# A gated linear attention and a maxout feed-forward on one core: all step lists and PSUM rooms in another order, with 154 runs of one tile shape on the array instead of 190

## The chip, the cores and the metric

The kernel runs on one core of a Trainium2 chip. The metric is the device time of one launch in microseconds (us); for the time before, it is the median of three runs. TensorE (PE in the profile, its weight loads PEld), VectorE (DVE), ScalarE (ACT), GpSimd (POOL) and SyncE (SP) each work through a list of their own in order, and wait for each other by semaphores.

## The reference

Two blocks follow each other. The first is a gated linear attention (4 batches, 8 heads, 768 steps, 48 features a head); its state has complex gates:

```
mag = sqrt(a_re^2 + a_im^2);  scale = min(mag, 0.999) / (mag + 1e-6);  a = (a_re, a_im) * scale
for t in range(S):
    S_re, S_im = a_re[t]*S_re - a_im[t]*S_im + outer(k[t], v[t]),  a_re[t]*S_im + a_im[t]*S_re
    y[t] = q[t] @ S_re
```

The second takes the heads side by side as 3072 tokens of 384 features:

```
h = max(max(x @ w1, x @ w2), x @ w3)      # 384 -> 768
out = h @ w_out                           # 768 -> 384
```

The activations are fp32. The four weight matrices come in as 64-bit floats.

## The kernel before, in words

The kernel is one program without loops. A text, `SCHEDULE`, lists some two thousand *words*, each a step and a group, such as `U01:5`. The program walks the list and records each word's instructions; a helper class ties each instruction to the one before it on its engine, so the order of the words is the order on every engine. (That is why nearly every row of the profile has one line, that of the helper.)

There are 12 groups. A group is 128 steps of two batches, x and y, so a word such as `Ax:5` belongs to batch x of group 5. The words by kind:

- Loads: `Lr Li Lk Lq Lv` (gates, keys, queries, values), on SyncE's queue.
- Gates, on ScalarE and VectorE: `sqr sqi add lnL expw expe lne relu Lnop abs addw lnw expL mulai mulw stt xor half atan turn`. They give each gate's log size and its angle. `Lnop`, `addw` and `Cd` add by a transfer in memory from GpSimd's queue, unless VectorE does it.
- Running sums over a group, on TensorE: `cs` of the angles and `sums` and `F` of the log sizes; `t nf af sa sb` make sines, `En Ek Eq f0..f3` exponentials out of them.
- `mk mq uk uq` scale the keys and queries, `tpk tpq` turn them on TensorE, `Kc Qc` copy the result out of PSUM, `Q1 Q2 KB QB QG` scale parts of it.
- Scores `A` and `B` on TensorE; `g0..g3` (VectorE) and `b0 b1` (ScalarE) write them through masks into `atm`. `dk` and `h0..h3` keep the state. `y` is the attention's output, and `x` copies it to where the second block reads it.
- Weights: twelve blocks are loaded (`WL`) and made into fp32 out of 64 bits: `Wa` copies the upper half into 16-bit floats (ScalarE or VectorE, as the list `OTHER` says), `We` joins in the lower bits (VectorE), and `Wg` adds the first matrix's negative to the two others. So the maximum is taken over two products and zero, and the first matrix's share goes into a matrix of its own (`T t M m`).
- Second block: up words `U01 U11 U02 U12` (9 products of 128x128 weights and 256 columns each; the small ones of group 0, with an x or y, have 6 of 128 columns), `u..` take the maximum. The down projection is done in seven half-size products `P1`..`P7` with sums of the operands `S1`..`S4` on VectorE, and `Px Py` for what is left; `r1 r6 r75 r57 ox oy` put the output together, `D` stores it.

TensorE's array is used in five tile shapes: 128x128 (up words, P, Px, the weights' products), 128x32 (A, B, y), 128x64 (`cs`), 64x64 (`F sums dk`) and 64x128 (`tpk tpq`). Words of one shape that stand behind each other in TensorE's list are called a run.

PSUM is divided into four rooms of two banks. `SLOTS` has a digit for each word that takes a room, in the order of the words; a word waits until the room's last user has been read. `QUARTERS` names words whose products are each made in four, 32 columns of the weights at a time, with the same columns streamed (for `cs`: in 32s instead of 64s):

```
def mmf(out, lhsT, rhs, **kw):
    for o in range(0, P, 32) if T["word"] in QUARTERS else ():
        mm(out=out[o:o + 32], lhsT=lhsT[:, o:o + 32], rhs=rhs, **kw)
    if T["word"] not in QUARTERS:
        mm(out=out, lhsT=lhsT, rhs=rhs, **kw)
```

In the kernel before, `QUARTERS` is empty.

Of the kernel before, what the change touches and what calls it, by code (L numbers as in the profile page):

```python
# [29 lines left out]
0624060202264204602604204624604602204600406204240620420460246260246202460246024062624640406204602602  # L30
6402466024240642460246026042064264064240246060206426040260046024240604204060420602640424062420242002
4202
"""

OTHER = set("""
Zf:0 Zg:0 afx:0 relu:1 Qcy:0 addw:2 Lnop:2 Wg8:0 u21y:0 addw:3 relu:4 afx:3 abs:4 Lnop:4 u01:2 xx:3 afy:4 afx:5 addw:6 u01:4 afx:6 afy:6 abs:7 relu:8 Kcy:6 afy:7 afx:7 relu:9 abs:9 u11:7 u01:7 afx:9 Kcx:9 xy:8 u11:8 Kcy:9 afy:10 abs:11 Kcx:10 Qcy:10 Kcy:11 Kcx:11 xy:11 u01:11 u11:11
""".split())

QUARTERS = set("""
""".split())  # L40

ROOMS = {0: "w1", 3: "w2", 6: "wo", 11: "w1", 1: "w2", 9: "H", 10: "S", 2: "H", 4: "S", 5: "H", 7: "S", 8: "H"}
# [927 lines left out]
```

## Time and profile before

| | before |
|---|---|
| median of 3 runs | 555.67 us (555.03 to 556.41) |
| profiled execution, its own time | 555.11 us |
| its span in the profile | 553.4 us |
| TensorE busy, share of the span | 524.8 us, 95% |
| VectorE | 470.8 us, 85% |
| ScalarE | 369.7 us, 67% |
| GpSimd | 70.7 us, 13% |
| products in the trace (passes; an fp32 product is two) | 10086 |

The span begins with the first instruction and ends with the last; 1.7 us of the profiled execution's time lie around it. A row of a group has the line, the engine, the operation, what it writes and reads, the count, the busy time and the mean of one in ns, and the idle time before such instructions with what ended it. In a row of the timeline stand start and length in us, the engine, the form and how many of it were merged. A busy PE row includes the time in which a product waits in the array's pipeline, so the starts of two rows tell more than the lengths.

### The profile page before, as it was taken

To read this page: it belongs to the slowest core of one execution; us is meant where nothing else is said; L and a number is where in the kernel's file an instruction comes from. 1 tells how busy PE (TensorE), PEld (TensorE's weight loads), DVE (VectorE), ACT (ScalarE), POOL (GpSimd) and SP (SyncE) were. 2 spreads that over 40 slices of the span, in tenths; PEclk is the share of its full clock that TensorE was granted. 3 is DMA by queue.
4 is the path that set the end of the run, shared out by engine and by line. 5 is a ranking of instruction groups with operands and counts; after the bars stand their busy time and mean duration, and the time that the engine had idled before them with its cause. 6 is when DMAs were issued, how large, how long until landed. Compare 5 with 4: busy or idle time off the path is not lost.

```text
span 553.4 us, 22672 instructions
## 1 busy us (share of the span) xinstructions
PE 524.8 (95%) x10086; PEld 449.1 (81%) x10086; DVE 470.8 (85%) x728; ACT 369.7 (67%) x653; POOL 70.7 (13%) x117
## 2 busy tenths in 40 slices
PE   3579899999999999999999999999999999999996
...
GB/s 227 272 236 195 168 125 80 51 128 63 108 40 122 69 67 53 61 44 89 80 111 58 35 102 129 64 91 52 67 123 18 32 107 70 3 31 2 31 1 28
...
## 3 DMA queue, kind: packets, MB, share of 16 engines
...
q14 instruction: 18, 0.15, 0.1%
...
## 4 chain that ended last, share of the span: by engine, by line
PE 84%; ACT 5%; SPq 5%; DVE 2%; DMA 2%; issue 1%; DVEq 0%; ACTq 0%
PE up L107 33%; PE op L107 24%; PE y L107 7%; PE A L107 5%; SPq L107 5%; PE tp L107 4%; PE dk L107 3%; PE cs L107 3%; PE sums L107 2%; PE F L107 2%; PE B L107 1%; DMA ar<-in_a_re_dram 1%; ACT L L107 1%; ACT L107 1%; DMA ai<-in_a_im_dram 1%
## 5 line engine op out<-in xcount | busy, mean ns | idle before, releaser
L107 PE MATMUL up<-xhx,w 128*128 128x256 f32 x792 | 177.0, 382 | 0.1
L107 PEld LDWEIGHTS up<-xhx,w 128*128 128x128 f32 x792 | 148.9, 190 | 21.2 <-PE B L107 0.3
L107 ACT ACT_TABLE_LOAD x49 | 62.9, 1283 | 1.6 <-PEq L954 0.8
L107 ACT COPY atm<-B 32x128 f32<-32x128 f32 x96 | 24.5, 255 | 36.6 <-DVE atm L107 19.1
L107 PE MATMUL op<-wo,xhx 128*128 128x192 f32 (+1 forms) x220 | 48.6, 364 | 0.0
L107 DVE TENSOR_TENSOR Q<-Q,f 112x1024 f32<-112x1024 f32 (+1 forms) x48 | 45.4, 953 | 2.1 <-ACT Q L107 1.2
L107 POOL DMA_DIRECT2D ar<-nf x40 | 34.6, 1304 | 60.5 <-DVE ar L107 49.2
L107 ACT ACTIVATE f<-F 48x232 f32<-48x232 f32 x96 | 34.4, 359 | 10.3 <-PE F L107 6.3
L107 PEld LDWEIGHTS op<-wo,xhx 128*128 128x128 f32 x220 | 36.5, 190 | 4.8 <-issue 0.8
L107 PE MATMUL y<-atm,vb 128*32 128x64 f32 x1152 | 39.3, 222 | 0.1
L107 PE MATMUL y<-QG,g 112*32 112x64 f32 x1408 | 38.1, 219 | 0.3 <-issue 0.3
L107 PEld LDWEIGHTS y<-atm,vb 128*32 128x32 f32 x1152 | 32.5, 110 | 5.4 <-issue 2.9
L107 PEld LDWEIGHTS y<-QG,g 112*32 112x32 f32 x1408 | 34.9, 110 | 0.5 <-issue 0.5
L107 DVE TENSOR_TENSOR ot<-ot,op 128x384 f32<-128x384 f32 (+1 forms) x56 | 25.6, 465 | 10.7 <-PE op L107 6.4
L107 PE MATMUL op<-wo,strassen 128*128 128x192 f32 x176 | 33.0, 331 | 0.0
L107 POOL DMA_DIRECT2D Ln<-e x9 | 8.3, 923 | 192.0 <-ACT e L107 73.7
L107 DVE COPY_PREDICATED atm<-masko,A 128x256 f32<-128x256 uint8 x72 | 31.3, 436 | 1.7
L107 PE MATMUL op<-w,strassen 128*128 128x192 f32 x176 | 32.2, 329 | 0.0
L107 PE MATMUL A<-Q,K 112*32 112x80 f32 x1536 | 31.6, 234 | 0.2 <-DVE Q L107 0.2
L107 PEld LDWEIGHTS A<-Q,K 112*32 112x32 f32 x1536 | 27.3, 110 | 3.0 <-issue 1.6
L107 ACT COPY Q<-tp 112x1024 f32<-112x1024 f32 x22 | 22.3, 1015 | 10.7 <-PE tp L107 10.6
L107 PEld LDWEIGHTS op<-wo,strassen 128*128 128x128 f32 x176 | 28.8, 190 | 0.8
(149 smaller groups left out, 1071.5 us busy)
## 6 DMA issues: line engine op xcount, KB each, us to landing
...
```

Source lines behind the costliest of these rows:

```text
L107: ins = f(*a, **kw)
```

## The change

No step is changed: the same words are recorded, each once. What changes is data at the head of the file: the order of the words in `SCHEDULE`; the rooms in `SLOTS`; the words that `OTHER` gives to the other of two engines (among them seven of the twelve copies `Wa`, now on VectorE); and `QUARTERS`, which now names 51 words. With the new order TensorE's list falls into 154 runs of one shape instead of 190. `ROOMS` and all functions stay as they are.

```
 SCHEDULE = """
-Lrx:0 sqr0:0 Lix:0 sqi0:0 add0:0 lnL0:0 expe0:0 expw0:0 lne0:0 relu0:0 Z0:0 Z1:0 WL0:0 Liy:0 Wa0:0 sqi1:0 Zf:0 Lry:0 sqr1:0 WL3:0 Lqy:0 Lry:1 WL6:0 WL9:0 Lkx:0
...
-P7:11 r75:11 ox:11 P4:11 Dx:11 r57:11 oy:11 Dy:11
+Zg:0 Lix:0 sqi0:0 Lrx:0 sqr0:0 Zf:0 add0:0 lnL0:0 xor0:0 Liy:0 sqi1:0 expe0:0 Lry:0 sqr1:0 WL0:0 WL3:0 expw0:0 relu0:0
...
+Py:11 P4:11 S1:11 S2:11 P6:11 P5:11 P2:11 S4:11 P3:11 Dx:10 r1:11 Dy:10 r6:11 r75:11 r57:11 ox:11 Dx:11 oy:11 Dy:11
 SLOTS = """
-0240624024202406402024604642064262624062046420640426240260620406404624624620620260264064262464046042
...
+0246246206246026042624046460206402064020462046240620462462024620642064260426042060460642620462640260
...
 OTHER = set("""
-Zf:0 Zg:0 afx:0 relu:1 Qcy:0 addw:2 Lnop:2 Wg8:0 u21y:0 addw:3 relu:4 afx:3 abs:4 Lnop:4 u01:2 xx:3 afy:4 afx:5 addw:6 u01:4 afx:6 afy:6 abs:7 relu:8 Kcy:6 afy:7 afx:7 relu:9 abs:9 u11:7 u01:7 afx:9 Kcx:9 xy:8 u11:8 Kcy:9 afy:10 abs:11 Kcx:10 Qcy:10 Kcy:11 Kcx:11 xy:11 u01:11 u11:11
+Zg:0 Zf:0 Z1:0 Wa3:0 afx:0 ty:0 relu:1 Wa6:0 Qcx:0 Wa9:0 Wa11:0 Wa10:0 addw:2 Wa7:0 xy:0 Wa8:0 Wg8:0 afx:1 afy:2
+u21y:0 relu:3 addw:3 xx:1 xy:1 Qcy:2 addw:4 relu:5 afx:4 abs:5 r1:2 addw:5 Kcx:4 u11:3 tx:5 afx:5 xx:4 Qcx:5 afy:6
+abs:7 addw:7 xy:5 u01:5 Qcy:6 tx:7 afy:7 r1:5 xx:6 xy:6 afy:8 afx:8 abs:9 u11:7 ty:9 afy:9 r1:7 Kcx:9 ty:10 relu:11
+abs:11 addw:11 Lnop:11 tx:11 afy:11 afx:11 r1:9 xy:10 Qcy:11 xy:11 r1:10 u11:11 u01:11 r1:11
 """.split())
 QUARTERS = set("""
+csx:0 csy:0 csx:1 csx:2 Px:3 Py:3 csx:6 P6:4 Px:4 Py:6 Px:6 P3:6 csx:9 csy:9 P7:7 P5:7 P2:7 P4:7 U11:8 csx:10 Px:8
+csy:10 P7:8 U12:9 U02:9 csy:11 Px:9 P6:9 csx:11 P4:9 P2:9 P3:9 Py:10 Px:10 P2:10 P4:10 Px:11 P6:10 U12:11 U11:11 P3:10
+U02:11 U01:11 P7:11 P1:11 Py:11 P4:11 P6:11 P5:11 P2:11 P3:11
 """.split())
```

More of the change, by code (lines that the diff above doesn't have):

```diff
@@ new lines @@
+Zg:0 Lix:0 sqi0:0 Lrx:0 sqr0:0 Zf:0 add0:0 lnL0:0 xor0:0 Liy:0 sqi1:0 expe0:0 Lry:0 sqr1:0 WL0:0 WL3:0 expw0:0 relu0:0
+lne0:0 add1:0 lnL1:0 expe1:0 Lnop0:0 Fx:0 lne1:0 sumsx:0 abs0:0 pw0:0 half0:0 expw1:0 f0x:0 relu1:0 f1x:0 xor1:0
+Lnop1:0 Ekx:0 Eqx:0 abs1:0 Z0:0 Wa0:0 f3x:0 lnw0:0 expL0:0 Z1:0 Wa3:0 Enx:0 We3:0 We0:0 half1:0 mulai0:0 mulw0:0 pw1:0
+lnw1:0 stt0:0 expL1:0 mulw1:0 atan0:0 mulai1:0 stt1:0 turn0:0 Lix:1 Lqx:0 mqx:0 atan1:0 turn1:0 csx:0 csy:0 Lry:1
+Lrx:1 WL6:0 sqr:1 Lkx:0 mkx:0 tx:0 nfx:0 afx:0 Liy:1 sqi:1 add:1 sbx:0 sax:0 ukx:0 WL9:0 Lky:0 WL11:0 lnL:1 f2x:0
@@ new lines @@
+uqx:0 ty:0 expe:1 relu:1 tpkx:0 Kcx:0 Wa6:0 lne:1 tpqx:0 Qcx:0 Fy:0 Wa9:0 QGx:0 nfy:0 sumsy:0 f0y:0 expw:1 xor:1
+kEnx:0 We9:0 Lry:2 We6:0 WL10:0 Eny:0 abs:1 T1:0 half:1 Q2x:0 Eky:0 Eqy:0 Wa11:0 Wa10:0 We10:0 mky:0 f1y:0 Lnop:1 CL:0
+f2y:0 f3y:0 pw:1 Lvy:0 t1:0 T0:0 t0:0 We11:0 T2:0 M0:0 M1:0 t2:0 M2:0 WL1:0 Lqy:0 Liy:2 Lix:2 Lrx:2 Lvx:0 afy:0 lnw:1
+expL:1 mulw:1 say:0 Cdx:0 mulai:1 sqi:2 mqy:0 Wa1:0 QBx:0 stt:1 sby:0 atan:1 We1:0 Q1x:0 Ax:0 KBx:0 sqr:2 add:2 lnL:2
+m0:0 m1:0 uky:0 uqy:0 Cdy:0 turn:1 WL2:0 Wa2:0 g0x:0 g1x:0 Wg1:0 tpky:0 tpqy:0 Qcy:0 We2:0 Wg2:0 Kcy:0 g2x:0 Q1y:0
@@ new lines @@
+Q2y:0 xor:2 csy:1 Z2:0 g3x:0 WL4:0 Wa4:0 We4:0 Wg4:0 kEny:0 dkx:0 expe:2 relu:2 csx:1 tx:1 nfx:1 expw:2 abs:2 half:2
+Cdx:1 Ay:0 ty:1 nfy:1 Z4:0 h1x:0 Lix:3 Bx:0 b0x:0 b1x:0 yx:0 Z3:0 WL5:0 Wa5:0 Lqx:1 Lkx:1 WL7:0 afy:1 xx:0 U01x:0
+addw:2 g0y:0 QBy:0 Cdy:1 g1y:0 h2x:0 g2y:0 We5:0 Wg5:0 dky:0 lnw:2 expL:2 g3y:0 KBy:0 mulw:2 By:0 h3x:0 sby:1 U11x:0
+b0y:0 b1y:0 QGy:0 mulai:2 stt:2 Lqy:1 h1y:0 yy:0 say:1 Wa7:0 h2y:0 h3y:0 xy:0 We7:0 Wg7:0 atan:2 u01x:0 turn:2 sumsx:1
+Ekx:1 sumsy:1 Eqy:1 mqy:1 u11x:0 WL8:0 mkx:1 Wa8:0 Eqx:1 We8:0 Eky:1 uqy:1 lne:2 U01y:0 Wg8:0 U02y:0 u01y:0 Enx:1
@@ new lines @@
+Eny:1 csy:2 ty:2 nfy:2 u02y:0 Fx:1 mqx:1 Lky:1 mky:1 f3x:1 f0x:1 afx:1 sax:1 uky:1 afy:2 sbx:1 U12y:0 U11y:0 u11y:0
+f1x:1 f2x:1 u12y:0 ukx:1 uqx:1 U21y:0 U22y:0 u21y:0 u22y:0 tpky:1 Kcy:1 tpkx:1 Kcx:1 kEnx:1 tpqx:1 tpqy:1 Lnop:2
+kEny:1 Liy:3 Lvx:1 Liy:4 Lvy:1 Oy:0 Qcx:1 QBx:1 Q2x:1 dkx:1 Q1x:1 oy:0 Qcy:1 sqi:3 Fy:1 f0y:1 f3y:1 J3:0 QGx:1 Ax:1
+h0x:1 h1x:1 h2x:1 h3x:1 Lky:2 g0x:1 g1x:1 KBx:1 f2y:1 f1y:1 Q1y:1 g2x:1 g3x:1 h0y:1 Q2y:1 U21x:0 u21x:0 Fx:2 f2x:2
+f0x:2 f1x:2 sumsx:2 dky:1 h1y:1 f3x:2 Ekx:2 Enx:2 Lix:4 Eqx:2 h2y:1 Lry:3 Lrx:3 sqr:3 add:3 xor:3 Bx:1 b0x:1 b1x:1
@@ new lines @@
+U12x:0 u12x:0 lnL:3 relu:3 U22x:0 u22x:0 U02x:0 h3y:1 Ay:1 Lqx:2 Lqy:2 Lkx:2 Lvy:2 KBy:1 csx:2 yx:1 QBy:1 mqx:2 tx:2
+nfx:2 u02x:0 expw:3 By:1 Ox:0 QGy:1 Lrx:4 g0y:1 g1y:1 expe:3 afx:2 abs:3 half:3 g2y:1 g3y:1 mkx:2 addw:3 say:2 b1y:1
+xx:1 b0y:1 sax:2 sbx:2 sby:2 lnw:3 uqx:2 h0x:2 J1:0 Lry:4 yy:1 xy:1 Lvx:2 expL:3 sumsy:2 Fy:2 ukx:2 mulai:3 ox:0 Eky:2
+mky:2 Eny:2 Eqy:2 mqy:2 U11:1 Dy:0 lne:3 Lnop:3 f3y:2 f2y:2 f0y:2 f1y:2 uqy:2 tpqx:2 u11:1 uky:2 tpqy:2 tpkx:2 tpky:2
+mulw:3 stt:3 Qcx:2 Qcy:2 atan:3 Kcy:2 kEny:2 Q1x:2 kEnx:2 Kcx:2 KBx:2 Cdx:2 QBx:2 Cdy:2 turn:3 QGx:2 U01:1 Q2y:2 U12:1
@@ new lines @@
+u01:1 U02:1 u12:1 S3:1 Q2x:2 sqi:4 sqr:4 add:4 Q1y:2 u02:1 csy:3 lnL:4 csx:3 ty:3 nfy:3 tx:3 h0y:2 Ax:2 afy:3 nfx:3
+sbx:3 Ay:2 Dx:0 S1:1 g0x:2 g1x:2 g2x:2 g3x:2 Bx:2 QBy:2 expe:4 P7:1 P1:1 b1x:2 b0x:2 g0y:2 S2:1 afx:3 sax:3 say:3 Px:1
+P5:1 Lqy:3 dkx:2 relu:4 sby:3 g1y:2 g2y:2 J2:0 g3y:2 P6:1 h1x:2 h2x:2 Lrx:5 yx:2 r1:1 KBy:2 h3x:2 By:2 Lix:5 Lry:5
+Lvy:3 Lkx:3 expw:4 abs:4 r6:1 xor:4 r75:1 r57:1 QGy:2 half:4 S4:1 J4:0 Py:1 xx:2 P2:1 addw:4 b0y:2 b1y:2 sumsx:3 Enx:3
+sumsy:3 Eqy:3 dky:2 Eky:3 Ekx:3 Lvx:3 Lky:3 lnw:4 Eny:3 h1y:2 mky:3 P4:1 P3:1 ox:1 mqy:3 oy:1 h2y:2 yy:2 Eqx:3 xy:2
@@ new lines @@
+Fx:3 f2x:3 uky:3 Fy:3 f0y:3 f1y:3 f2y:3 expL:4 U01:2 f3y:3 f3x:3 f1x:3 lne:4 f0x:3 Lqx:3 mqx:3 uqx:3 tpqx:3 uqy:3
+mkx:3 h3y:2 ukx:3 mulai:4 mulw:4 u01:2 stt:4 Qcx:3 Q1x:3 QBx:3 atan:4 tpqy:3 tpky:3 kEny:3 tpkx:3 Kcx:3 Cdy:3 Cdx:3
+turn:4 Kcy:3 Lnop:4 sqr:5 Liy:5 sqi:5 Lvx:4 U02:2 KBx:3 U11:2 Bx:3 Q2x:3 kEnx:3 u02:2 Qcy:3 add:5 h0x:3 Q2y:3 S3:2
+h0y:3 Ax:3 g0x:3 g1x:3 g2x:3 u11:2 g3x:3 Lqx:4 b0x:3 b1x:3 QGx:3 U12:2 dkx:3 dky:3 sumsx:4 Ekx:4 Eqx:4 u12:2 S1:2
+Q1y:3 h1x:3 h1y:3 KBy:3 S2:2 h2x:3 h2y:3 P1:2 P7:2 P5:2 Lky:4 Enx:4 h3y:3 h3x:3 QBy:3 lnL:5 expe:5 csy:4 ty:4 csx:4
@@ new lines @@
+tx:4 Lry:6 Dx:1 mqx:4 nfy:4 expw:5 relu:5 sby:4 nfx:4 afx:4 sbx:4 abs:5 Ay:3 yx:3 By:3 afy:4 g0y:3 g1y:3 g2y:3 xx:3
+sax:4 say:4 P6:2 Py:2 P4:2 S4:2 Px:2 P2:2 Lkx:4 mkx:4 g3y:3 Dy:1 lne:5 r1:2 r6:2 QGy:3 Lqy:4 Lnop:5 addw:5 b0y:3 lnw:5
+ukx:4 b1y:3 uqx:4 r75:2 r57:2 expL:5 P3:2 ox:2 oy:2 Lrx:6 Liy:6 xor:5 half:5 mulw:5 yy:3 xy:3 tpkx:4 tpqx:4 Qcx:4
+mulai:5 stt:5 Fx:4 f3x:4 f0x:4 sumsy:4 Eqy:4 mqy:4 uqy:4 Dx:2 Eky:4 mky:4 Kcx:4 Eny:4 Dy:2 U01:3 U02:3 Lix:6 f1x:4
+sqr:6 uky:4 U11:3 Lvy:4 u01:3 sqi:6 kEnx:4 f2x:4 QBx:4 Q1x:4 tpky:4 tpqy:4 KBx:4 Q2x:4 xor:6 add:6 u02:3 kEny:4 atan:5
@@ new lines @@
+lnL:6 expe:6 u11:3 Qcy:4 Kcy:4 Ax:4 U12:3 QGx:4 g0x:4 Cdx:4 Cdy:4 turn:5 g1x:4 g2x:4 h0x:4 g3x:4 Bx:4 b0x:4 Fy:4 f1y:4
+u12:3 S3:3 Lky:5 b1x:4 f3y:4 f2y:4 f0y:4 dkx:4 Fx:5 h1x:4 h2x:4 f0x:5 h3x:4 f1x:5 h0y:4 S1:3 csy:5 csx:5 f2x:5 f3x:5
+tx:5 nfx:5 dky:4 sumsx:5 ty:5 Eqx:5 Enx:5 P1:3 P5:3 KBy:4 h1y:4 h2y:4 QBy:4 h3y:4 nfy:5 Q1y:4 afx:5 Q2y:4 Ekx:5 expw:6
+yx:4 xx:4 QGy:4 S2:3 Px:3 Py:3 By:4 Ay:4 g0y:4 sbx:5 afy:5 g1y:4 S4:3 g2y:4 P7:3 P6:3 sax:5 relu:6 abs:6 say:5 sby:5
+g3y:4 P2:3 P3:3 half:6 Lqx:5 Lrx:7 Liy:7 Lry:7 h0x:5 mqx:5 uqx:5 b1y:4 b0y:4 yy:4 xy:4 sumsy:5 Lqy:5 r1:3 addw:6
@@ new lines @@
+tpqx:5 lnw:6 Eky:5 Qcx:5 Lqx:6 Lvx:5 r6:3 r75:3 r57:3 mky:5 Lix:7 expL:6 Q2x:5 mulw:6 mulai:6 stt:6 lne:6 P4:3 sqi:7
+Liy:8 Lkx:5 ox:3 QGx:5 oy:3 uky:5 U01:4 u01:4 Q1x:5 Eqy:5 mqy:5 U02:4 u02:4 atan:6 mkx:5 Eny:5 Lnop:6 sqr:7 add:7
+uqy:5 ukx:5 QBx:5 turn:6 U11:4 U12:4 u11:4 u12:4 tpkx:5 tpqy:5 tpky:5 kEnx:5 Kcx:5 Kcy:5 csy:6 ty:6 Ax:5 dkx:5 Qcy:5
+S3:4 nfy:6 S1:4 g0x:5 KBx:5 h1x:5 g1x:5 Fy:5 f2y:5 f3y:5 P1:4 f1y:5 P7:4 P5:4 f0y:5 Q2y:5 g2x:5 Bx:5 Q1y:5 Ay:5 S2:4
+afy:6 lnL:7 relu:7 expe:7 lne:7 g3x:5 b1x:5 b0x:5 csx:6 P6:4 tx:6 h0y:5 expw:7 Lvy:5 Lry:8 QBy:5 g0y:5 g1y:5 nfx:6
@@ new lines @@
+g2y:5 KBy:5 afx:6 sax:6 Px:4 g3y:5 yx:5 By:5 b0y:5 xx:5 sbx:6 b1y:5 say:6 S4:4 kEny:5 QGy:5 Lvx:6 Dx:3 Lix:8 Dy:3
+Lrx:8 Lkx:6 Py:4 P4:4 Lky:6 abs:7 xor:7 r1:4 r6:4 sby:6 addw:7 lnw:7 P3:4 P2:4 sumsy:6 r75:4 dky:5 ox:4 r57:4 oy:4
+sumsx:6 Eky:6 expL:7 Eqx:6 Ekx:6 h1y:5 yy:5 Enx:6 mulw:7 Lqy:6 xy:5 Eqy:6 Lnop:7 Eny:6 mqy:6 mqx:6 mulai:7 uqx:6
+half:7 mkx:6 Cdy:6 Lqx:7 Fy:6 f3y:6 Fx:6 f3x:6 sqi:8 xor:8 f2x:6 f1x:6 f1y:6 f0y:6 f0x:6 U11:5 U01:5 mky:6 u11:5 stt:7
+Lix:9 Lvy:6 uqy:6 ukx:6 f2y:6 tpqx:6 uky:6 u01:5 Qcx:6 tpqy:6 tpky:6 atan:7 Qcy:6 Lqy:7 tpkx:6 Kcx:6 Lvy:7 QBx:6 Q1y:6
@@ new lines @@
+Cdx:6 turn:7 Q1x:6 Q2x:6 Kcy:6 Dy:4 Lkx:7 Lry:9 Dx:4 sqr:8 add:8 Q2y:6 lnL:8 expe:8 U02:5 u02:5 U12:5 csy:7 csx:7 Ax:6
+KBx:6 relu:8 kEnx:6 expw:8 abs:8 u12:5 tx:7 nfx:7 Ay:6 S1:5 addw:8 ty:7 nfy:7 g0x:6 g1x:6 dkx:6 h1x:6 h2x:6 g2x:6
+g0y:6 g3x:6 sby:7 h3x:6 g1y:6 S2:5 half:8 P1:5 P5:5 Bx:6 QBy:6 b0x:6 KBy:6 afy:7 g2y:6 Lvx:7 r1:5 lnw:8 b1x:6 g3y:6
+Px:5 Py:5 P2:5 P4:5 kEny:6 QGx:6 P6:5 S4:5 By:6 b1y:6 expL:8 yx:6 b0y:6 S3:5 mulai:8 P7:5 dky:6 xx:6 P3:5 r6:5 r75:5
+QGy:6 afx:7 sbx:7 h1y:6 h2y:6 yy:6 sax:7 lne:8 Lnop:8 Cdy:7 r57:5 oy:5 h3y:6 ox:5 sumsx:7 Eqx:7 Enx:7 sumsy:7 Eky:7
@@ new lines @@
+Fx:7 xy:6 U12:6 mqx:7 Ekx:7 Eny:7 mkx:7 f3x:7 f0x:7 Eqy:7 uqx:7 Liy:9 ukx:7 Lrx:9 mqy:7 f2x:7 Lky:7 mulw:8 stt:8
+Lix:10 mky:7 f1x:7 Dx:5 tpqx:7 tpkx:7 Qcx:7 Q2x:7 U11:6 Lkx:8 say:7 kEnx:7 QGx:7 QBx:7 Kcx:7 h0x:7 Q1x:7 uky:7 U01:6
+Lky:8 KBx:7 uqy:7 u11:6 u12:6 sqi:9 xor:9 sqr:9 add:9 dkx:7 h1x:7 h2x:7 u01:6 atan:8 Cdx:7 Fy:7 f1y:7 Fx:8 f0y:7 lnL:9
+U02:6 f0x:8 turn:8 f3y:7 f3x:8 h3x:7 u02:6 f1x:8 f2x:8 h0x:8 f2y:7 tpqy:7 tpky:7 Lvx:8 Qcy:7 Kcy:7 csx:8 csy:8 h0y:7
+kEny:7 tx:8 nfx:8 ty:8 nfy:8 Lqx:8 Q1y:7 sumsy:8 S1:6 sumsx:8 Enx:8 Eqx:8 Dy:5 Eqy:8 Ekx:8 Lqy:8 dky:7 Q2y:7 S2:6
@@ new lines @@
+Liy:10 Lrx:10 Ax:7 g0x:7 g1x:7 g2x:7 afy:8 Eky:8 Eny:8 expe:9 lne:9 Py:6 Px:6 Bx:7 h1y:7 P4:6 afx:8 P2:6 g3x:7 b1x:7
+S3:6 b0x:7 mky:8 h2y:7 QBy:7 h3y:7 P5:6 KBy:7 S4:6 Ay:7 expw:9 g0y:7 g1y:7 g2y:7 mqx:8 yx:7 relu:9 xx:7 P3:6 By:7
+sby:8 sax:8 say:8 QGy:7 mkx:8 abs:9 addw:9 mqy:8 g3y:7 b1y:7 b0y:7 sbx:8 P7:6 P6:6 P1:6 r1:6 uqx:8 r6:6 ukx:8 yy:7
+xy:7 r75:6 half:9 Cdy:8 ox:6 Lry:10 r57:6 oy:6 Dy:6 tpqx:8 Qcx:8 QBx:8 lnw:9 Lvy:8 uky:8 Lky:9 uqy:8 Q1x:8 expL:9
+mulai:9 Q2x:8 mulw:9 stt:9 Lvx:9 Lkx:9 U01:7 u01:7 tpkx:8 Kcx:8 Lqx:9 tpky:8 tpqy:8 QGx:8 kEny:8 KBx:8 Fy:8 f1y:8
```

34 lines of the change are left out of this document (30 added, 4 removed).

## The prediction

> **What bounds the kernel now.** I read the page first: busy time by engine, the slices, and the chain that ended last.
>
> ```profile
> span 553.4 us, 22672 instructions
> ...
> PE 524.8 (95%) x10086; PEld 449.1 (81%) x10086; DVE 470.8 (85%) x728; ACT 369.7 (67%) x653; POOL 70.7 (13%) x117
> ...
> PE   3579899999999999999999999999999999999996
> ...
> PE 84%; ACT 5%; SPq 5%; DVE 2%; DMA 2%; issue 1%; DVEq 0%; ACTq 0%
> ```
>
> TensorE is busy in nine tenths or more of every slice after the first few, and the chain lies on it for 84%. Next the busy time by stretch, whose columns are length, then PE, PEld, DVE, ACT, POOL busy, the granted clock, and DMA:
>
> ```profile
> 0.00:60.00 60.00, 39.46 (x462) 25.25 (x466) 42.63 (x69) 55.02 (x95) 24.16 (x62) 0.89 0.94 233
> 60.00:100.00 40.00, 37.65 (x896) 32.13 (x892) 36.91 (x59) 35.10 (x65) 7.32 (x8) 1.00 0.57 106
> 100.00:200.00 100.00, 99.41 (x2161) 85.03 (x2154) 95.82 (x149) 74.72 (x130) 13.37 (x16) 1.00 0.41 80
> 200.00:300.00 100.00, 99.93 (x1887) 87.85 (x1887) 88.69 (x136) 75.76 (x127) 6.76 (x8) 1.00 0.40 76
> 300.00:400.00 100.00, 99.78 (x2094) 87.41 (x2089) 92.05 (x145) 73.37 (x132) 10.83 (x13) 1.00 0.39 74
> 400.00:500.00 100.00, 100.00 (x1964) 87.93 (x1964) 90.34 (x135) 52.71 (x98) 8.28 (x10) 1.00 0.27 54
> 500.00:553.00 53.00, 48.58 (x676) 43.46 (x667) 24.31 (x41) 3.06 (x11) 0.00 (x0) 1.00 0.05 16
> ```
>
> So there are three stages. In the first 100 us PE idles 20.5 + 2.4 = 22.9 us, and ScalarE (55.02 of the first 60) sets the pace. From 100 to 500 PE idles 0.6 + 0.1 + 0.2 + 0.0 = 0.9 us: there the time is simply what PE takes for its words in the order given. The last 53 us hold 4.4 us of idleness, all at the end. A new order of the same words can gain in the middle only by making the words themselves cheaper on PE.
>
> **What a change of tile shape costs.** PE's timeline near the end, where it waits for nothing, gives that: start, time, form, passes (a product in fp32 is two passes, so an up word of 9 products is 18).
>
> ```profile
> 485.82 0.66 PE L107 MATMUL tp<-ident,uq 64*112 64x64 f32 x16
> 486.31 1.06 PE L107 MATMUL tp<-ident,uk 64*112 64x64 f32 x32
> 487.21 0.61 PE L107 MATMUL tp<-ident,uq 64*112 64x64 f32 x16
> 487.75 11.92 PE L107 MATMUL up<-xhx,w 128*128 128x256 f32 x54
> 499.60 1.14 PE L107 MATMUL dk<-vb,uk 64*64 64x48 f32 x64
> 500.67 1.31 PE L107 MATMUL A<-Q,K 112*32 112x80 f32 x64
> 501.92 4.15 PE L107 MATMUL up<-xhx,w 128*128 128x256 f32 x18
> 506.00 1.31 PE L107 MATMUL A<-Q,K 112*32 112x80 f32 x64
> ...
> 508.98 1.46 PE L107 MATMUL op<-w,strassen 128*128 128x192 f32 x8
> 510.28 1.46 PE L107 MATMUL op<-wo,strassen 128*128 128x192 f32 x8
> 511.67 0.32 PE L107 MATMUL y<-atm,vb 128*32 128x64 f32 x8
> ...
> 513.28 0.48 PE L107 MATMUL B<-QB,KB 112*32 112x32 f32 x32
> ...
> 519.08 0.32 PE L107 MATMUL y<-atm,vb 128*32 128x64 f32 x8
> ...
> 520.80 1.57 PE L107 MATMUL op<-wo,strassen 128*128 128x192 f32 x8
> 522.20 15.70 PE L107 MATMUL up<-xhx,w 128*128 128x256 f32 x72
> 537.74 1.46 PE L107 MATMUL op<-wo,xhx 128*128 128x192 f32 x8
> ```
>
> Four up words with no change around them take 537.74 - 522.20 = 15.54 us, 3.885 each. One that stands alone between other shapes takes 506.00 - 501.92 = 4.08. A run of 128x128 words therefore costs 0.195 us for its two ends, however long it is (the three words from 487.75 to 499.60 take 11.85, which is 3 x 3.885 + 0.195). A y word followed by its own shape takes 513.28 - 511.67 = 1.61, one followed by a 128x128 word 520.80 - 519.08 = 1.72: 0.11 for a 128x32 run. The turns (tp, 64x128): first 0.49, middle two 0.45 each, last 0.54: 0.13 a run. For 64x64 and 128x64 runs I take 0.15 and 0.07, between nothing and the dearest of these, 0.195.
>
> **The change, part by part.** I counted the runs in both lists by the shape that each word's products have (the title's 190 and 154 are the runs):
>
> - 128x128: 61 to 54, 7 x 0.195 = 1.4 us
> - 128x32: 52 to 40, 12 x 0.11 = 1.3 us
> - 64x128: 24 to 17, 7 x 0.13 = 0.9 us
> - 64x64: 39 to 35, 4 x 0.15 = 0.6 us
> - 128x64: 14 to 8, 6 x 0.07 = 0.4 us
>
> Together 4.6 us less on PE, with 4.0 to 5.4 as bounds from the two prices that no quoted row shows. All of it lies on the path, since PE idles 0.9 us in the middle 400.
>
> Quarters: 11 of the 51 words are running sums (cs, from two column tiles to four); the others are 7 up words, 22 products P and 11 Px or Py, each now four products 32 columns wide where one of 128 stood, on four column groups. No word of before has that with 192 or more columns. The nearest row is y, which runs on four 32-column groups with all 128 rows: 112 passes in 1.61 us, 28 for each group, 57.5 ns each. A full-width pass takes 15.54 / 72 = 215.8 ns for 256 columns and 1.30 / 8 = 162.5 for 192 (508.98 to 510.28), so 0.833 ns for a column and 2.5 fixed; y's 64 columns would be 53.3, and 4.2 is fixed. A quartered pass should cost 1.7 ns more than a whole one. 7 x 18 + 22 x 8 + 11 x 2 = 324 passes: +0.5 us. The other four-group row, A at 506.00 (64 passes of 80 columns up to B at 507.19, 16 a group, 74 ns where 66.7 are columns), would give 7.7 fixed, so +1.7 us. I take 0.5, because y has all 128 rows as the quarters have; bounds 0 to 1.7. The running sums I cost at nothing, -0.5 to +0.5: the columns streamed in each group stay the same.
>
> ```profile
> L107 PEld LDWEIGHTS y<-atm,vb 128*32 128x32 f32 x1152 | 32.5, 110 | 5.4 <-issue 2.9 <-ACT atm L107 1.0 <-ACT e L107 0.5
> L107 ACT ACTIVATE xhx<-xhx 128x768 f16<-128x768 bf16 x4 | 4.3, 1076 | 0.0
> L107 DVE TENSOR_SCALAR ar<-ar 128x768 int32<-128x768 int32 x11 | 6.1, 555 | 0.1
> L107 DVE TENSOR_SCALAR xhx<-up 128x768 f32<-128x768 f32 x7 | 6.7, 957 | 11.5 <-PE up L107 11.5
> L107 ACT COPY K<-tp 112x1024 f32<-112x1024 f32 x18 | 18.1, 1013 | 9.4 <-PE tp L107 9.3
> L107 ACT COPY xhx<-y 128x384 f32<-128x384 f32 x19 | 9.1, 481 | 13.6 <-PE y L107 13.5
> ```
>
> A 32-column weight load lasts 110 ns, yet y starts a pass every 1.61 / 112 = 14.4 ns, or every 57.5 in one group: the loads lie under the passes of the other groups and of their own. Here the Trainium skill speaks against the change: "TensorE: Matmul & The Clock Gate", Part 3, says that a weight load overlaps a running matmul only if the row group differs, and the four quarters share all rows. The y rows disagree; what it would make of the time is the third rival.
>
> The start, first 100 us: the new list gives 7 of the 12 conversion copies (Wa3, 6 to 11) to VectorE. On ScalarE they are 1.076 each, 7.5 us, and ScalarE's 55.0 of the first 60 becomes 47.5. On VectorE no such copy was seen: between 0.555 (one-input work in SBUF) and 0.957 (the same out of PSUM); I take 0.957, because input and output are strided 16-bit, not packed. That is +6.7, and VectorE's 42.6 becomes 49.3. The busier of the two falls by 5.7 us, which would be the whole gain if nothing else stood in the chain. But the loads (DMA 0.94 busy in this stretch), PE's own steps and the queue additions stand in it and stay as long. I take a quarter, -1.5 us, with -5.7 and +6.7 (all that VectorE got lies on the path) as ends. The load order changes on SyncE's queue as well: the gates' inputs of group 1 go ahead of three weight blocks, which serves the same chain.
>
> The middle: the lists put some pairs closer together. PE's work between a turn and the scores that need its copy is at least 8.1 us in before and 1.7 in group 5 of after; the copy is 1.013. Between an output word and the up words that need its features it falls from 1.2 to 0.6; that copy is 0.481. Each still fits if its engine is free, with 0.1 to 0.7 to spare. VectorE gets at least the copies' 6.7 us more (470.8 to some 478 of 550). I add 0.7 us of waits to the 0.9, bounds 0 and 3.
>
> The end:
>
> ```profile
> 545.55 1.46 PE L107 MATMUL op<-w,strassen 128*128 128x192 f32 x8
> 547.05 1.41 DVE L107 TENSOR_TENSOR ot<-ot,op 128x384 f32<-128x384 f32 x3 [2.50 <-PE op L107]
> 548.25 1.57 PE L107 MATMUL op<-w,xhx 128*128 128x192 f32 x8 [1.23 <-DVE ot L107]
> ...
> 549.85 0.62 DVE L107 TENSOR_TENSOR ot<-ot,op 128x192 f32<-128x192 f32 x2 [1.39 <-PE op L107]
> ```
>
> P4, the last product, waits 1.23 us for VectorE's additions to release the accumulator. In the new list P3 comes last and P4 far ahead; its operand sum S4 is made while P2 runs, which is 1.3 like every product P, so no such wait is left. But after P3 VectorE has a 384-wide addition ahead of the two halves of 549.85 (0.47, the third part of the 1.41 at 547.05), and one more output transfer stands ahead of the last. Net -0.6, bounds -1.4 and +0.5.
>
> Sum, against the profiled execution's 555.11 us (1.7 around its span): -4.6 + 0.5 - 1.5 + 0.7 - 0.6 = -5.5, so 549.6. That execution lies 0.56 below the median of the three runs, 555.67. I put the forecast between the two bases, at **549.9 us**.
>
> **The rivals.**
> 1. *The waits take it back.* VectorE is already at 95.8 of 100 us between 100 and 200; with its start fuller it may still be behind there, and the closer pairs then show. Each engine does what the lists say, so 3 us more of waits in the middle and none of the start's gain give 549.6 + 2.3 + 1.5 = 553.4; with all of the bounds of quarters 555. For it: the 1.7 and 0.6 us distances. Against: the middle idles 0.9 us with VectorE just as full. 12%.
> 2. *Slower: the conversion copies cost VectorE much more than 0.957.* If strided 16-bit writing takes twice as long, 1.9, seven copies add 6.6 us to the engine that then sets the start, all on the path as the start's gain goes: 549.6 + 1.5 + 6.6 = 557.7. It decides from about 1.65 each on (5.5 us over seven is 0.8 above 0.957). For it: no row shows VectorE writing in such strides. Against: ScalarE, which does, needs 1.076 by its row, and VectorE's plain work on as many elements 0.957. 8%.
> 3. *Slower: the quarters' weight loads are not hidden.* 324 passes x 110 ns = 35.6 us, so about 585. Against it stand the 1152 y passes of the row. By the page's rule named above it would be so. 2%.
> 4. *The start gains more,* half to all of the 5.7: 547 down to 545.4. 15%, faster as the forecast is.
>
> My forecast's own case, between 547 and 552.5, has 63%. The changes themselves are there: the runs are counted in the programs, so the change does what it says.
>
> **Range and chances.** A measurement here tells 0.3%, 1.7 us. 546.0 to 555.5 leaves out the second and third rivals and the ends of the first and fourth. Faster by over 0.3% (below 554.0): the own case, the fourth, and a third of the first, 0.82. Within 0.3%: the rest of the first, 0.08. Slower: the second and the third, 0.10.
>
> **What would show it.** Up words unbroken at 3.885 and quartered ones at 3.9 to 4.0 (right) or 5 and more (third rival). PE busy a few us lower in sum, its idle time before 100 us at 21 or 22, and under 2 from 100 to 500. The conversion copies on VectorE under 1.0. No wait before the last products. The forecast is wrong if PE's idle time before 100 us passes 27, or between 100 and 500 passes 5.

## The result, and the profile after

| | before | after |
|---|---|---|
| median (four runs each, on one chip) | 555.53 us (555.03 to 556.41) | 551.01 us (550.24 to 551.49) |
| ratio | | 0.9916, interval 0.9897 to 0.9934 |
| profiled execution, its span | 555.11, 553.4 us | 550.57, 548.8 us |

The change makes the kernel 4.5 us faster; 549.9 had been forecast. The head of the page after, with the third section's row of the instruction queue (packets, MB, share of the DMA engines), which matters further on:

```profile
span 548.8 us, 24794 instructions
...
PE 520.1 (95%) x11146; PEld 443.1 (81%) x11146; DVE 479.7 (87%) x755; ACT 363.6 (66%) x633; POOL 76.2 (14%) x114
...
q8 instruction: 87, 1.43, 1.0%
```

PE has 1060 passes more than before (the quarters) and yet is busy 4.7 us less. The busy time by stretch after, columns as in the prediction:

```profile
0.00:60.00 60.00, 37.31 (x522) 25.04 (x526) 49.09 (x80) 50.87 (x88) 33.02 (x64) 0.90 0.91 219
60.00:100.00 40.00, 39.39 (x842) 34.30 (x838) 36.73 (x59) 29.78 (x58) 6.44 (x8) 0.90 0.72 141
100.00:200.00 100.00, 100.00 (x2135) 86.84 (x2134) 95.89 (x150) 76.30 (x129) 12.45 (x15) 1.00 0.39 76
200.00:300.00 100.00, 99.66 (x1990) 87.28 (x1991) 92.57 (x140) 69.93 (x117) 6.54 (x8) 1.00 0.40 75
300.00:400.00 100.00, 99.15 (x2235) 86.20 (x2229) 93.21 (x156) 76.30 (x132) 10.32 (x13) 1.00 0.36 69
400.00:500.00 100.00, 100.00 (x2317) 85.16 (x2307) 88.26 (x135) 57.89 (x101) 7.47 (x9) 1.00 0.25 51
500.00:548.00 48.00, 44.54 (x1150) 38.26 (x1148) 23.92 (x42) 2.52 (x9) 0.00 (x0) 1.00 0.06 19
```

PE idles 22.7 + 0.6 = 23.3 us before 100 us (22.9 in before) and 0.0 + 0.3 + 0.9 + 0.0 = 1.2 us from 100 to 500 (0.9 in before). So the start gained nothing, the middle stayed full, and what was won, apart from the end, is shorter work on PE. VectorE's load in the first 60 us is the 49 that was forecast, though by luck (the copies bring 4.2 us and not 6.7; the rest is other work); ScalarE fell to 50.9, not to 47.5.

One column needs a second look: the granted clock from 60 to 100 us is 0.90, and was 1.00 before. These are the rows from 60 to 65 us, after and then before, and PE's timeline of a small up word in both:

```profile
60.00:65.00 5.00, 4.40 (x88) 4.16 (x84) 4.74 (x9) 4.17 (x6) 4.27 (x6) 0.50 1.07 251
60.00:65.00 5.00, 4.76 (x160) 3.96 (x152) 4.90 (x7) 4.97 (x8) 1.26 (x1) 0.99 0.17 25
```

```profile
62.65 2.93 PE L210 MATMUL up<-ot,w 128*128 128x128 f32 x12 [0.60 <-ACT ot L210]
65.50 1.95 PE L210 MATMUL dk<-vb,uk 64*64 64x48 f32 x64
...
62.53 1.61 PE L107 MATMUL up<-ot,w 128*128 128x128 f32 x12
64.07 0.56 PE L107 MATMUL sums<-Ln,mid 64*64 64x192 f32 x8
```

The same 12 passes take 65.50 - 62.65 = 2.85 us after and 64.07 - 62.53 = 1.54 before. After, PE has half the clock for 10.2 us, from 58.1 to 68.3; before, for 3.4 us from 56.6 on. (An earlier stretch at half clock, between 16 and 36 us, adds up to 10.2 us in both.) That is longer work, and no idle time shows it. PE had been busy for only 4.0 of the 8 us ahead of it; whether that brought the clock down was not tried.

PE's timeline after shows two places of quartered work (form 128x32):

```profile
451.27 0.61 PE L210 MATMUL tp<-ident,uk 64*112 64x64 f32 x16
451.80 4.09 PE L210 MATMUL up<-xhx,w 128*32 128x256 f32 x72
455.71 1.29 PE L210 MATMUL A<-Q,K 112*32 112x80 f32 x64
...
526.81 7.99 PE L210 MATMUL up<-xhx,w 128*32 128x256 f32 x144
534.58 1.52 PE L210 MATMUL op<-w,strassen 128*32 128x192 f32 x32
```

Two quartered up words take 534.58 - 526.81 = 7.77 us, 3.885 each, as whole ones do: the quarters cost nothing. And a quartered up word ahead of a word A takes 455.71 - 451.80 = 3.91 us, where a whole one between other shapes took 4.08. That is the gain from the saved changes of shape, seen in one word. Last, the end after:

```profile
541.72 1.52 PE L210 MATMUL op<-wo,xhx 128*32 128x192 f32 x32
...
543.02 1.52 PE L210 MATMUL op<-wo,strassen 128*32 128x192 f32 x32
544.58 1.08 DVE L210 TENSOR_TENSOR ot<-ot,op 128x384 f32<-128x384 f32 x3 [0.27 <-PE op L210]
545.16 1.30 SPq L210 DMA_DIRECT2D out_dram<-ot  x3
```

P3 starts 1.30 us behind P2, so no wait is left ahead of the last product. From its start to the span's end it is 548.8 - 543.02 = 5.78 us; from P4's start in before it was 553.4 - 548.25 = 5.15.

### The profile page after: what moved, and what is told of

Same layout as the page of the kernel before. It is cut to its first block, busy times and chain, and to the rows that moved or that the text cites. A ratio compares the mean times of both kernels' runs of the same rounds, so it can differ in the third digit from the quotient of the medians.

```text
span 548.8 us, 24794 instructions
## 1 busy us (share of the span) xinstructions
PE 520.1 (95%) x11146; PEld 443.1 (81%) x11146; DVE 479.7 (87%) x755; ACT 363.6 (66%) x633; POOL 76.2 (14%) x114
## 4 chain that ended last, share of the span: by engine, by line
PE 86%; DVE 5%; POOL 3%; SPq 2%; issue 2%; DMA 1%; ACT 0%; DVEq 0%; POOLq 0%
PE up L210 35%; PE op L210 24%; PE y L210 7%; PE A L210 5%; PE tp L210 4%; PE dk L210 4%; PE sums L210 3%; PE cs L210 3%; POOL KB L210 2%; SPq L210 2%; PE F L210 1%; PE B L210 1%; DVE w L210 1%; DVE atm L210 1%; DMA ar<-in_a_re_dram 1%
## 5 line engine op out<-in xcount | busy, mean ns | idle before, releaser
L210 PE MATMUL up<-xhx,w 128*128 128x256 f32 (+1 forms) x1170 | 177.9, 381 | 0.2 <-ACT xhx L210 0.2
L210 PEld LDWEIGHTS up<-xhx,w 128*128 128x128 f32 (+1 forms) x1170 | 143.4, 156 | 25.4 <-ACT Q L210 0.3
L210 PE MATMUL op<-wo,xhx 128*32 128x192 f32 (+3 forms) x406 | 49.6, 373 | 0.2 <-DVE nf L210 0.2
L210 POOL DMA_DIRECT2D ar<-nf x40 | 34.8, 1337 | 89.6 <-DVE ar L210 62.2
L210 PEld LDWEIGHTS y<-atm,vb 128*32 128x32 f32 x1152 | 34.3, 112 | 5.3 <-issue 3.6
L210 PEld LDWEIGHTS op<-wo,xhx 128*32 128x32 f32 (+1 forms) x406 | 34.9, 141 | 4.5 <-issue 1.6
L210 PE MATMUL op<-w,strassen 128*32 128x192 f32 (+1 forms) x344 | 33.0, 329 | 0.0
L210 PE MATMUL op<-wo,strassen 128*32 128x192 f32 (+1 forms) x320 | 32.6, 326 | 0.0
L210 POOL DMA_DIRECT2D Ln<-e x10 | 10.8, 1078 | 149.7 <-ACT e L210 130.3
L210 PEld LDWEIGHTS op<-wo,strassen 128*32 128x32 f32 (+1 forms) x320 | 28.7, 142 | 1.0
L210 ACT ACTIVATE L<-L 128x768 f32<-128x768 f32 (+1 forms) x28 | 21.7, 774 | 11.4 <-DVE L L210 11.1
```

The lines of the kernel that those rows point to most:

```text
L210: ins = f(*a, **kw)
```

## The experiments

A sum of all words frames them. Every word of both lists gets its unbroken time and each run of one shape a price, both fitted to the runs that begin between 105 and 535 us in the two traces: 0.20 for a run of 128x128, 0.11 for 128x32, 0.14 for 64x64, 0.15 for 64x128 and for 128x64. Half of all runs come out within 2 ns of it. The last price can be read directly, after:

```profile
75.43 0.87 PE L210 MATMUL cs<-w,upto 128*64 128x192 f32 x8
76.23 0.56 PE L210 MATMUL F<-cuts,Ln 64*48 64x29 f32 x32
...
337.90 1.52 PE L210 MATMUL cs<-w,upto 128*64 128x192 f32 x16
339.35 0.56 PE L210 MATMUL sums<-Ln,mid 64*64 64x192 f32 x8
```

One running sum between other shapes takes 0.80 us, two in a row 1.45: 0.65 a word, and 0.15 for the run. The rest of PE's time is waiting. By this sum, the 36 runs fewer save 5.2 us. Waiting up to 105 us (with the time to the first product and with what half the clock costs) is 34.8 instead of 33.4 us. From there on, P4's wait at the end aside, it is 1.9 in both.

### The masks earlier

In the new list GpSimd writes its masks (`CL`) while VectorE is fullest. The group's rows of after, with VectorE's conversion copies:

```profile
L210 POOL TENSOR_SCALAR_AFFINE_SELECT KB<-KB 128x128 f32<-128x128 f32 x2 | 6.5, 3229 | 0.1
...
L210 DVE TENSOR_SCALAR xhx<-w 128x768 f16<-128x768 bf16 x2 | 1.2, 606 | 0.0
...
L210 DVE TENSOR_SCALAR xhx<-strassen 128x768 f16<-128x768 bf16 x2 | 1.2, 594 | 0.0
```

The two selects take 6.5 us there (the first 5.5, the second 1.0), in before 1.1. Transfers that GpSimd issues stand behind them, and the second group's gates wait for these. So I moved the masks one step ahead of the wait:

```
-... mky:0 f1y:0 Lnop:1 CL:0
+... mky:0 f1y:0 CL:0 Lnop:1
```

> The changed kernel with one word moved: CL (GpSimd makes the masks) stands before Lnop:1 again, so that GpSimd makes them in the first 20 us, as it did in the kernel before. Theory: in the changed kernel CL runs from 29.4 to 45.1 us, in VectorE's busiest time, and holds back the additions Cd, for which turn:1 waits 2.1 us on VectorE, and KBx another 0.8; VectorE has no other gap there, so the start moves forward by these 2.9 us and the kernel takes 547.5 to 549 where the changed one takes 551.0. Rival: VectorE's own work sets the start and the wait is made up before TensorE is dense; then the time stays within 0.5 us of 551.0.

Measured: 551.25 us, ratio to before 0.9917 (0.9888 to 0.9946). The selects did become short, but not the time:

```profile
L210 POOL TENSOR_SCALAR_AFFINE_SELECT KB<-KB 128x128 f32<-128x128 f32 x2 | 1.1, 574 | 0.1
```

PE's idle time up to 100 us is 23.1, as good as after's 23.3. The first word y started 0.7 us earlier (58.95 instead of 59.66 us). The second was 0.9 us ahead (68.80 instead of 69.67) and then lost it in one stop within the word:

```profile
68.80 0.42 PE L210 MATMUL y<-atm,vb 128*32 128x64 f32 x15
69.87 0.24 PE L210 MATMUL y<-atm,vb 128*32 128x64 f32 x1 [0.65 <-issue]
```

By the end of the word it was level with after again. So the slow selects hold the start by less than 1 us and not by the 2.9 expected, and in this profiled execution even that was lost. The stop is of the kind that the borders of instruction blocks make (below): it ends 1.4 us after a block has landed.

### The copies back on ScalarE

```
 OTHER = set("""
-Zg:0 Zf:0 Z1:0 Wa3:0 afx:0 ty:0 relu:1 Wa6:0 Qcx:0 Wa9:0 Wa11:0 Wa10:0 addw:2 Wa7:0 xy:0 Wa8:0 Wg8:0 ...
+Zg:0 Zf:0 Z1:0 afx:0 ty:0 relu:1 Qcx:0 addw:2 xy:0 Wg8:0 ...
```

> The changed kernel with the seven conversion copies (Wa3, 6 to 11) on ScalarE again, all else as changed. They took 0.60 us each on VectorE and 1.08 on ScalarE. Theory: the masks, not VectorE's work, hold the start of the changed kernel up to 49.5 us, so taking 4.2 us off VectorE gains little, and ScalarE, now the fuller one, loses up to 3.4 us more: 551 to 555. Rival: VectorE's queue sets the start; then the time falls by 1 to 3 us, to 548 to 550.

Measured: 555.93 us, ratio to before 1.0012 (0.9989 to 1.0034): 4.9 us slower than after, the whole gain, and outside both answers that I had set. PE's timeline shows the first running sums in this run and then in after:

```profile
23.07 2.79 PE L207 MATMUL cs<-w,upto 128*32 128x192 f32 x32 [7.46 <-DVE w L207]
```

```profile
20.11 2.44 PE L210 MATMUL cs<-w,upto 128*32 128x192 f32 x32 [4.50 <-DVE w L210]
```

They start 3.0 us later, and by 100 us PE has idled 27.8 us, 4.5 more. In the new order the copies' place is worth 5 us.

### The copies on VectorE in the old order

```
 OTHER = set("""
-Zf:0 Zg:0 afx:0 ... u11:11
+Zf:0 Zg:0 afx:0 ... u11:11 Wa3:0 Wa6:0 Wa9:0 Wa11:0 Wa10:0 Wa7:0 Wa8:0
```

> The kernel before with the seven conversion copies (Wa3, Wa6 to Wa11) moved from ScalarE to VectorE, its list as it is. TensorE's instructions and borders are unchanged. Theory (ScalarE sets the pace of the first 60 us; the copies' place is worth about 5 us, and the changed list's first group loses it again): 550 to 552 us. Rival (VectorE is then as late as ScalarE was, the copies bring something only together with the changed order): 554.5 to 556 us.

Measured: 554.73 us over 12 runs, beside 554.70 for before; ratio 0.9994 (0.997 to 1.0017). The first stretch of its profile:

```profile
0.00:60.00 60.00, 39.79 (x518) 26.10 (x518) 45.94 (x75) 52.40 (x92) 24.87 (x62) 0.89 0.95 234
```

ScalarE falls from 55.0 to 52.4, VectorE rises from 42.6 to 45.9, and PE is busy 39.8 instead of 39.5. The rival held: the move alone brings nothing that can be measured (1.7 us would still lie within the interval). So the prediction's separate term for it was the wrong way to count. The new order needs the copies on VectorE so as not to lose 5 us; it isn't faster in the start through them.

### No quarters

```
 QUARTERS = set("""
-csx:0 csy:0 ... P3:11
 """.split())
```

Without them the new list has 191 runs of one shape, one more than the old one. All 36 that are saved come from the quarters, none from the order alone.

> The changed kernel with QUARTERS empty and all lists as they are. Counted in its list, it has 191 runs of one shape instead of 154, as many as the kernel before. Theory: the change of order alone saves no runs and the quarters save all of them at no price of their own; by the prices of the prediction (0.195 a 128x128 run, 0.11 a 128x32 run, 0.07 a 128x64 run; 17, 11 and 9 more) TensorE needs 5.2 us more, 555.5 to 556.5, which is the time of the kernel before. Rival: the quartered words cost as much as they save, or the waits behind them take it up: 551 to 553.

Measured: 568.88 us, ratio to before 1.024 (1.0205 to 1.0276). Both answers that I had set were missed. The 37 runs that it has more than the changed list explain about 6 of the 17.9 us above after; fitted alone, this trace gives the same prices within 0.02 us. PE's timeline shows what the rest is made of:

```profile
220.27 0.70 PE L208 MATMUL cs<-w,upto 128*64 128x192 f32 x5
222.49 1.19 PE L208 MATMUL cs<-w,upto 128*64 128x192 f32 x11 [1.52 <-issue]
223.61 0.60 PE L208 MATMUL dk<-vb,uk 64*64 64x48 f32 x29
```

In the middle of a word PE stands still with nothing that the profile could name as a reason ("issue"). Between 100 and 545 us the start of a pass lies more than 0.45 us behind the start of the pass before it at 12 places, 13.2 us together. I call these gaps; after has 2 with 1.4 us, before 1 with 0.6. Ten of the 12 end 1.25 to 1.5 us after a packet of the instruction queue has landed.

### Quarters in the whole old list

```
 QUARTERS = set("""
+csx:1 csy:1 U11:1 U01:1 U02:1 U12:1 csx:3 csy:3 P5:1 ... P7:11 P4:11
 """.split())
```

(163 words; the list then has 130 runs.)

> The kernel before with nothing but QUARTERS changed: 163 words (up words, products P, Px and Py, running sums) are made in quarters wherever that saves a change of shape, counted by the prices measured; 130 runs instead of 190. Theory: quarters cost nothing and every saved change is off TensorE's path, 11.2 us by those prices: 544 to 546. Rival 1: VectorE, busy for 471 us, becomes late and waits take half of it back: 549 to 551. Rival 2: so many more products (163 words with four times the instructions) cost their own time in issue or fetching: 553 and more.

Measured: 571.71 us, ratio 1.029 (1.024 to 1.034), as the second rival had it. Here PE has 20 gaps, 21.1 us together, and 19 of them end in the same way behind a packet of the instruction queue.

### Where the borders of the instruction blocks fall

The queue's packets are blocks of 16 KB: 87 of them for 2 x 11146 instructions of PE after, 79 for 2 x 10086 in before. That is 256 instructions each. An fp32 product is four instructions (two passes, two weight loads), so a block holds 64 products. The theory: PE stands still where a block's border falls into a dense stretch of instructions. It can be tried without touching any work. In the first 9 us PE has nothing to do but wait for the first data; there, n tiny products (32x8, out of a constant tile, read by nobody) push all later borders by 4n instructions:

```
+    fill = const.tile([P, 32], FP, name="fill")
+    dve.memset(fill, 1.0)
...
+    room = psum.tile([P, 2, 512], FP, tag="ps0", name="pad")
+    for _ in range(n):
+        mm(out=room[0:32, 0, 0:8], lhsT=fill[:, 0:32], rhs=fill[:, 0:8], start=True, stop=True)
     blocks = weight_blocks()
```

> The changed kernel with 16 tiny products (32x8, out of a constant tile) on TensorE ahead of its first word, where TensorE waits for the first transfers anyway: 64 more instructions, which push the borders of the 16 KB blocks of the instruction queue by a quarter of a block against the work. Theory (TensorE stalls where a block's border falls into a dense stretch of instructions, and the lists that stand fast are those whose borders fall well): some gaps of 0.8 to 2 us on TensorE that end 1.2 to 1.7 us after a block has landed, 553 to 566 us. Rival (the stalls seen in the list without quarters come from that list's own waits, borders don't matter): 550.0 to 552.0 us, no gap more than the 3 (1.8 us) of the changed kernel.

> The same with 32 tiny products: borders pushed by half a block. Theory: 553 to 566 us, with gaps at other places than with 16. Rival: 550.0 to 552.0 us.

> The kernel before with the same 32 tiny products ahead of its first word. Theory: 557 to 570 us, slower by the gaps at the new borders. Rival: 554.5 to 556.0 us, as the kernel before.

> The changed kernel without quarters (568.9 us, of which about 12 us are gaps at borders) with the same 32 tiny products. Theory: the gaps move or go: off 568.9 by 3 us or more, and about 556.5 if all of them go. Rival: 568 to 570 us.

> The changed kernel with 64 tiny products ahead of its first word: by the counts (2121 instructions more for 8 blocks between the list without quarters and the changed one, about 4 instructions a product) some 256 instructions, one whole block, so each border falls where it fell before against the work. Theory (only the border's place counts): 550 to 553 us, at most some 3 gaps after 100 us, where 16 and 32 products gave 15 and 17 gaps. Rival (added products disturb TensorE's stream as such, by their number): 570 us or more.

> The changed kernel with 4 tiny products ahead of its first word: 16 instructions, a sixteenth of a block. It asks how wide the good place of the borders is: 0 and 64 products gave 551.0 and 551.5 us, 16 and 32 gave 574.9 and 568.4. Wide (the stretches that hold a border for the good lists are long): 550.0 to 552.0 us with 3 or 4 gaps after 100 us. Narrow (a few instructions decide): 554 to 562 us with 6 to 12 gaps.

Measured, with PE's idle time from 100 to 500 us:

| kernel | products added | borders moved by | time, us | ratio to before | PE idle, 100 to 500 us |
|---|---|---|---|---|---|
| after | 0 | 0 | 551.01 | 0.9916 (0.9897 to 0.9934) | 1.2 |
| after | 4 | 1/16 block | 556.21 | 1.0016 (0.9997 to 1.0036) | 3.7 |
| after | 16 | 1/4 | 574.88 | 1.0367 (1.032 to 1.0413) | 12.9 |
| after | 32 | 1/2 | 568.37 | 1.0263 (1.0208 to 1.0319) | 12.1 |
| after | 64 | 1 | 551.52 | 0.9938 (0.9917 to 0.996) | 2.2 |
| before | 32 | 1/2 | 579.48 | 1.0424 (1.0381 to 1.0467) | 16.5 |
| after, no quarters | 0 | | 568.88 | 1.024 (1.0205 to 1.0276) | 9.9 |
| after, no quarters | 32 | 1/2 | 569.36 | 1.0263 (1.0231 to 1.0295) | 8.0 |

The theory held where it was sharpest: a whole block is harmless, a half or a quarter of one costs 17 and 24 us. That is more than the ranges that I had set (up to 566, and 570 for before). The idle time from 100 to 500 us comes from the stretches; here they are for 32 and then for 64 products:

```profile
100.00:200.00 100.00, 97.41 (x2114) 84.28 (x2116) 93.96 (x147) 73.50 (x124) 10.49 (x14) 1.00 0.37 72
200.00:300.00 100.00, 95.78 (x1823) 83.26 (x1816) 86.83 (x132) 66.39 (x117) 7.84 (x10) 1.00 0.36 68
300.00:400.00 100.00, 98.31 (x2148) 84.85 (x2147) 91.94 (x149) 73.57 (x125) 10.12 (x12) 1.00 0.39 75
400.00:500.00 100.00, 96.42 (x2391) 81.76 (x2390) 85.38 (x136) 60.10 (x106) 8.33 (x10) 1.00 0.27 55
```

```profile
100.00:200.00 100.00, 99.97 (x2132) 86.55 (x2131) 95.07 (x149) 75.45 (x128) 12.44 (x15) 1.00 0.39 75
200.00:300.00 100.00, 99.67 (x2018) 87.30 (x2017) 92.61 (x140) 69.90 (x117) 6.76 (x8) 1.00 0.40 75
300.00:400.00 100.00, 99.16 (x2237) 86.18 (x2232) 93.20 (x156) 76.30 (x132) 10.10 (x12) 1.00 0.37 69
400.00:500.00 100.00, 99.04 (x2281) 84.16 (x2270) 86.62 (x133) 57.88 (x101) 7.47 (x9) 1.00 0.26 50
```

One of the gaps with 32 products, in PE's timeline, and the DMA view of the same core between 489 and 493 us:

```profile
491.46 0.22 PE L210 MATMUL y<-QG,g 112*32 112x64 f32 x2
491.48 0.22 PE L210 MATMUL y<-atm,vb 128*32 128x64 f32 x1
493.34 0.24 PE L210 MATMUL y<-QG,g 112*32 112x64 f32 x1 [1.64 <-issue]
```

```profile
q8 instruction: 1, 0.02, 1.5%
```

One packet was moved in these 4 us, and it took 1.5% of 16 engines' 64 us, 0.96 us. By its record it begins at 490.94 and lands at 491.92. The next y pass starts at 493.34, 1.42 later. In the lists that stall most, nearly every gap has this shape.

Which borders hurt can be counted from the same records. For each block fetched between 100 and 540 us I divided PE's instructions that started during the transfer by its time. Where a gap followed, it was about 85 to 130 in a microsecond (the means of twelve kernels); where none did, 28 to 56. The y words are the densest. Among after's 77 blocks 7 begin to move while y runs, and 9 of before's 69. With 16 products it is 11, with 32 it is 13, and 15 for before with 32. But the old list in quarters has 20 gaps with 10 of its 100 blocks in y. So the gaps go with dense stretches; that density decides each one isn't shown.

Two rows need a word more. With 4 products the gaps are 6 with 5.5 us and the time is 556.2, in the narrow answer's range: 16 instructions are enough to take the change's whole gain. And the list without quarters stayed at 569 with 32 products: its gaps fell from 13.2 to 9.4 us, but the start lost 2.1 us, and the 3 us that the theory asked for did not come. Where the rest went was not followed.

### The end with P4 last

```
-Py:11 P4:11 S1:11 S2:11 P6:11 P5:11 P2:11 S4:11 P3:11 Dx:10 r1:11 Dy:10 r6:11 r75:11 r57:11 ox:11 Dx:11 oy:11 Dy:11
+Py:11 S1:11 S2:11 P5:11 P6:11 P2:11 S4:11 P3:11 Dx:10 r1:11 Dy:10 r6:11 r75:11 r57:11 P4:11 ox:11 Dx:11 oy:11 Dy:11
```

> The changed kernel with the last products in the order of the kernel without the change but P4 at the very end, behind P3. Theory (the end is the last product's own chain, and one product after the weights' last wait is as good as another): 550.3 us, 0.6 to 0.8 us less. Rival (P3's longer chain of outputs sets the end as well): 551.0 us, within 0.3 us of the changed kernel.

Measured: 551.36 us, ratio to before 0.9937 (0.992 to 0.9954). On the same chip after with 64 products took 551.52. The rival held. The end of its timeline:

```profile
545.05 1.52 PE L210 MATMUL op<-w,xhx 128*32 128x192 f32 x32
546.61 1.08 DVE L210 TENSOR_TENSOR ot<-ot,op 128x384 f32<-128x384 f32 x3 [2.18 <-PE op L210]
547.19 1.30 SPq L210 DMA_DIRECT2D out_dram<-ot  x3
```

The span is 550.9, so the end takes 5.85 us from the last product's start, as with P3 last (5.78). P3 and P4 do equally well as the last product without a wait; 5.15 was short because P4 had waited while everything else was finished. No run of the study beat the changed kernel.

## Why the prediction was right, and where it was wrong

- **Changes of tile shape.** Forecast -4.6, by the prices of both traces -5.2. Right, and it carries the result. The term that was too small is the 128x64 run, 0.15 and not 0.07. The sum is read from the traces: no run isolates it, since whoever takes the quarters out moves the borders of the instruction blocks as well.
- **Quarters.** Forecast +0.5, measured 0: 3.885 and 1.30 us a word, as whole ones. The step that failed is the fixed time of a pass, 4.2 ns out of y. It is y's own; a quarter of 256 columns pays no more than a whole pass. The running sums cost nothing, as forecast: 0.65 us a word, 0.64 in quarters.
- **The third rival,** weight loads that aren't hidden, is out: 585 would have come of it. The Trainium skill's rule ("TensorE: Matmul & The Clock Gate", Part 3), that a weight load overlaps only with products in other row groups, doesn't hold here for products in four column groups: four quarters share all rows and lose nothing.
- **The start.** Forecast -1.5, measured +1.4 (idle time 23.3 us, not 21 to 22; the rest is not idle time). This is the term that was wrong, in sign too. The price of a copy on VectorE was also off, 0.60 us instead of 0.957, so VectorE got 4.2 us of work and not 6.7, which should have helped. What failed is the step "a quarter of the fall of the busier engine". It took the load off ScalarE as a gain by itself, and the rest of the new first group as harmless. The runs show that the move alone brings nothing in the old order and that the new order would lose 4.9 us without it. Of the reasons, the slow masks are worth less than 1 us, as far as the profile without them shows. In the trace after, PE idles between a first-group word and the next that needs it (0.96 us between A and B, 0.98 between B and y, 0.60 between y and the up word), where before had other words in between. And it has half the clock for 6.8 us longer than before, which the prediction left out: that up word alone takes 1.3 us more. How the 1.4 us divide between the two, and whether the first brings on the second, was not tried.
- **The middle.** Forecast +0.7, measured 0 by the sum of words; PE's idle time rose by 0.3. The closer pairs fit.
- **The end.** Forecast -0.6, measured -0.8: 1.4 us of waiting gone, 0.6 of it given back by the longer way out.

Together -5.2 + 1.4 - 0.8 = -4.6, beside 4.6 of span and 4.5 of median. The start's 2.9 us of error was for the larger part made good by the four other terms, each a little better than forecast, by luck and not by reasoning.

Four figures of the working don't come out of their own numbers. The changes of shape have 3.6 to 5.5 as bounds by the prices named, not 4.0 to 5.4. The second rival decides from 1.74 us a copy on, not 1.65. Half of the 5.7 us at the start gives 548.2, not 547. And 64 of y's 112 passes have 112 rows, not 128. None of them moves the forecast.

Something larger was missed. I argued that the middle could only change by what the words themselves cost. It can change by 20 us through the place of the instructions in memory, which no row of before shows, as its list has only one such gap. That the forecast held rests on the new list being as well placed as the old: four tiny products more at its head would have given 556.2, no gain, and sixteen 574.9, far outside the range.
